# Adding partial products by accumulating transfers instead of on VectorE, in a kernel of attention beside a gated feed-forward network

## The chip, the core and the metric

The kernel runs on one core of one Trainium2 chip. The core has a matrix engine (TensorE, PE in the profile, with its weight loads as PEld), a vector engine (VectorE, DVE), an engine for functions of one input (ScalarE, ACT), a general engine (GpSimd, POOL) and an engine that issues transfers (SyncE, SP). Each engine takes its instructions in order. Transfers (DMAs) are issued by SP or by POOL here and run on 16 DMA engines that all queues share. The metric is the time of one execution on the device in microseconds; lower is better.

## The reference

The output is the sum of three things: the input `x`, an attention with a memory, and a gated feed-forward network, both on the layer-normalised input. There are 2048 tokens of width 448, 16 heads of width 28, four segments of 512 tokens, and 1792 hidden units.

```python
g = sigmoid(beta)
for s in range(4):                                   # segments of 512 tokens
    logits = qs @ ks.T * scale + mask
    a_dot = softmax(logits) @ vs
    a_mem = (phi(qs) @ M) / (phi(qs) @ z + 1e-6)      # phi(t) = t + 1 where t > 0, else exp(t)
    outs.append(g * a_mem + (1.0 - g) * a_dot)
    M = M + phi(ks).T @ vs
    z = z + phi(ks).sum(tokens)
attention = concat(outs) @ wo
gated = (sigmoid(xn @ w_gate) * (xn @ w_up)) @ w_down
return x + attention + gated                          # xn = layernorm(x)
```

The mask adds -1e9 where the key's place is before the query's.

## The kernel before

**Arithmetic.** All large products take operands that are split into a high and a low part, so one product of depth 448 is 11 matmuls (`TERMS`) and one of depth 128 is three. `acc[b]` holds, for block `b` of 512 tokens, first the input and then the running sum of the output: four tiles (`t`) of 128 tokens by 448.

**Phase 1, the front (L251 to L486).** It normalises, projects to queries, keys and values, writes them to DRAM (`qd`, `vd`), builds the memory `M`, and computes the memory's part of the attention in `recall` (L352): its result `tb` goes to `md[b]` in DRAM by a transfer that POOL issues (L358). The first steps of the feed-forward network are already mixed in here. In the front the order of PE, ACT and DVE is the program's own (`FRONT`, L51).

**Phase 2, the feed-forward network beside the attention.** From here on only PE's order is written by hand (`MANUAL`, L50). The order of ACT, DVE, POOL and SP is chosen by the framework's scheduler when the program is built, and each then runs in that fixed order. PE alternates steps of two generators: `gated` and `attention`.

- `gated` (L147) walks over the hidden units in pairs of 128-wide slices (`f0` = 0, 2, ..., 12, seven pairs), and for each pair over the four blocks `b`. For one pair and block it makes four *slots*: gate and up product of each slice (L224, 11 matmuls each). After a slice's two products ACT and DVE form the hidden values `hh` (L232 to L237).
- `down` (L149) multiplies the two slices' `hh` by their down weights: for each of the four token tiles six matmuls (L154) into one PSUM bank, three for the first slice and then three for the second. Then DVE adds the bank to `acc` (L157). The four `down` of one pair and block are put in the list `todo` (L244) and one is taken after each slot, two slots late. The banks alternate between `pd` and one of the two `gu`, so one kind comes back every second `down`.
- Weights come by SP: `load_up` (L162) into `raw` (one buffer, 512 KB), `load_down` (L166) into `rawd` (two buffers, 224 KB each). `ready_up` (L170) and `ready_down` (L174) split them: ACT copies the high part (L82), DVE subtracts to get the low part (L83). A buffer is free for the next load once DVE has read it. `wdn` has four buffers in the pool `late`, which exists only after the front. So the first two `ready_down` are held back in `begin` (L188) and issued at L491. The dictionary `ahead` (L201 to L215) says after which block and slot the later loads and splits are issued.
- `attention` (L618) works on pairs of heads (`Pair`): PE makes scores (L522), ACT copies them out (L525), POOL masks (L534), DVE takes maxima (L537) and subtracts (L573), ACT takes the exponential (L574). `Unit.finish` (L593) multiplies four heads' weights by the values (L599), turns the result (L606) and weighs it (L125) into `on`. For segments after the first, POOL adds the memory's part `tb` (L611), which SP has loaded from `md` (`load_memory`, L588 to L591). POOL then issues the transfer of `on` to `od` (L612).

**Phase 3, the output projection (`project`, L653).** `od` is loaded, turned and multiplied by `wo`; DVE adds to `acc` (L685), and the sum is stored.

Of the kernel before, what the change touches and what calls it, by code (L numbers as in the profile page):

```python
# [9 lines left out]
F32 = mybir.dt.float32  # L10
F32R = mybir.dt.float32r
AF = mybir.ActivationFunctionType
ALU = mybir.AluOpType
# [3 lines left out]
P = 128  # L17
D = 448
# [3 lines left out]
NB = 4  # L22
L = 512
NT = 4
# [9 lines left out]
FG = 2  # L34
# [22 lines left out]
def kernel(  # L57
# [69 lines left out]
    qd = [dram.tile([2 * D, 2, L], F32, name=f"qd{b}") for b in range(NB)]  # L127
    fd = [dram.tile([D, L], F32, name=f"fd{b}") for b in range(NB)]
    vd = [dram.tile([P, NT, H * 32], F32, name=f"vd{b}") for b in range(NB)]
    md = [dram.tile([P, NT, D], F32, name=f"md{b}") for b in range(NB)]  # L130
    od = [dram.tile([P, NT, D], F32, name=f"od{b}") for b in range(NB)]

    mid = ctx.enter_context(tc.tile_pool(name="mid", bufs=3, reuse_waits="tile"))
# [12 lines left out]

    def gated():  # L147

        def down(b, hs, wd, t, tag="pd"):  # L149
            tok = slice(t * P, (t + 1) * P)  # L150
            mms = [(h[:, a, tok], wd[f][:, w, :]) for f, h in hs for a, w in ((0, 0), (0, 1), (1, 0))]
            pd = bank("pd", tag)
            for n, (l, r) in enumerate(mms):
                T.matmul(pd[:, :D], l, r, start=n == 0, stop=n == len(mms) - 1)  # L154
                if n == 2:
                    yield
            V.tensor_add(acc[b][:, t, :], pd[:, :D], acc[b][:, t, :])  # L157
            yield

        raw_up, raw_down, wgu, wdn = {}, {}, {}, {}  # L160

        def load_up(f):  # L162
            raw_up[f] = mid.tile([P, 1024], F32, name="raw", bufs=1)
            nc.sync.dma_start(raw_up[f], w_ffn[f][:, :1024])

        def load_down(f):  # L166
            raw_down[f] = mid.tile([P, D], F32, name="rawd", bufs=2)
            nc.sync.dma_start(raw_down[f], w_ffn[f][:, 1024:])

        def ready_up(f):  # L170
            wgu[f] = eight_k(F32R, "wgu")
            split_weights(wgu[f], raw_up[f].rearrange("p (c n) -> p c n", c=4))

        def ready_down(f):  # L174
            wdn[f] = late[0].tile([P, 2, D], F32R, name="wdn", bufs=4)
            split(wdn[f][:, 0, :], wdn[f][:, 1, :], raw_down[f])

        raw_o = {}

        def load_out(h):  # L180
            raw_o[h] = mid.tile([P, 1024], F32, name="raw", bufs=1)[:, :2 * D]
            nc.sync.dma_start(raw_o[h], w_o[:, 2 * D * h:2 * D * (h + 1)])

        def ready_out(h):
            wo[h] = eight_k(F32R, "wo").rearrange("p c n -> p (c n)")
            split(wo[h][:, :2 * D], wo[h][:, 2 * D:4 * D], raw_o[h])

        begin.append(lambda: (ready_down(0), ready_down(1)))  # L188
        load_up(0)
        yield  # L190
        ready_up(0)
        load_up(1)
        load_down(0)
        load_down(1)
        yield


        todo = [None, None]
        for f0 in range(0, NF, FG):

            ahead = {}  # L201
            if f0 == 0:
                ahead[0, 0] = lambda: ready_up(1)
            if f0 + FG < NF:
                ahead[0, 2] = lambda: load_up(f0 + 2)
                ahead[1, 2] = lambda: (ready_up(f0 + 2), load_down(f0 + 2))
                ahead[1, 3] = lambda: load_up(f0 + 3)
                ahead[2, 1] = lambda: (ready_down(f0 + 2), load_down(f0 + 3))
                ahead[3, 2] = lambda: ready_up(f0 + 3)
                ahead[3, 3] = lambda: ready_down(f0 + 3)  # L210
            else:

                ahead[0, 2] = lambda: load_out(0)
                ahead[1, 2] = lambda: (ready_out(0), load_out(1))
                ahead[3, 2] = lambda: ready_out(1)  # L215
            for b in range(NB):
                hs = []
                for f in range(f0, f0 + FG):
                    pgu = []
                    for side in range(2):  # L220
                        slot = 2 * (f - f0) + side
                        dst = bank("pgu", ("gu", "p")[side])
                        for n, (a, w) in enumerate(TERMS):
                            T.matmul(dst, wgu[f][:, w, side * P:(side + 1) * P], xs[b][:, a, :],  # L224
                                     start=n == 0, stop=n == len(TERMS) - 1)
                            if n in (3, 7):
                                yield
                        pgu.append(dst)
                        if side == 1:

                            sg = two_k("sg")
                            A.activation(sg, pgu[0], AF.Tanh, scale=0.5)  # L232
                            V.scalar_tensor_tensor(sg, sg, 1.0, pgu[1], op0=ALU.add, op1=ALU.mult)  # L233
                            hh = four_k(F32R, "hh")
                            A.activation(hh[:, 0, :], sg, AF.Copy, scale=0.5)  # L235
                            V.scalar_tensor_tensor(hh[:, 1, :], sg, 0.5, hh[:, 0, :].bitcast(F32),  # L236
                                                   op0=ALU.mult, op1=ALU.subtract)  # L237
                            hs.append((f, hh))
                        yield
                        if todo and f0 + b > 0:  # L240
                            yield from todo.pop(0) or ()
                        if (b, slot) in ahead:
                            ahead[b, slot]()
                todo += [down(b, hs, wdn, t, ("pd", "gu")[t % 2]) for t in range(NT)]  # L244
        rest.extend(todo)


# [3 lines left out]
    with tc.tile_pool(name="front", bufs=2) as sb, tc.manual_schedule(engines=FRONT):  # L251
# [100 lines left out]
        def recall(b, i, phi):  # L352
            tb = sb.tile([P, NT * HG, DH], F32, name="tb", bufs=2)
            n2 = bank("n2", ("m", "pd")[i % 2] if b < NB - 1 else "m")
            for t in range(NT):
                T.matmul(n2[:, t * P:(t + 1) * P], phi[:, t * P:(t + 1) * P], mst[b % 2][i], start=True, stop=True)  # L356
            weigh(sb, tb, n2, gate[:, HG * i:HG * (i + 1)], MEM_EPS)
            nc.gpsimd.dma_start(md[b][:, :, GW * i:GW * (i + 1)], tb.rearrange("p (t j) d -> p t (j d)", t=NT))  # L358

        raw = [four_k(F32, "wv_raw") for _ in range(2)]  # L360
        raw = [raw[t // 2][:, t % 2, :D] for t in range(4)]
# [215 lines left out]
    class Unit:  # L577
# [7 lines left out]
            self.vv = sb.tile([P, NT, HG * 32], F32, name="vv")  # L585
            nc.sync.dma_start(self.vv, vd[self.s][:, :, self.i * P:(self.i + 1) * P])

        def load_memory(self):  # L588
            if self.s > 0:
                self.tb = sb.tile([P, NT, GW], F32, name="tb")  # L590
                nc.sync.dma_start(self.tb, md[self.s][:, :, GW * self.i:GW * (self.i + 1)])  # L591

        def finish(self):  # L593

            s, i = self.s, self.i
# [11 lines left out]
            on = sb.tile([P, NT * HG, DH], F32, name="on")  # L607
            weigh(sb, on, n1, gate_n[:, HG * i:HG * (i + 1)], 0.0)
            o3 = on.rearrange("p (t j) d -> p t (j d)", t=NT)
            if s > 0:  # L610
                G.tensor_add(o3, o3, self.tb)  # L611
            nc.gpsimd.dma_start(od[s][:, :, GW * i:GW * (i + 1)], o3)  # L612
            yield

    pairs = [Pair(n) for n in range(NB * H // 2)]
# [2 lines left out]
    def attention():  # L618
# [5 lines left out]
        for u in range(len(units) + 1):  # L624
            for n in range(2):
                run[n] = pairs[2 * u + n].scores() if u < len(units) else iter(())
            for k, which in enumerate(SLOT):
# [15 lines left out]
                if which == 2 and u > 0:  # L643
                    fin = units[u - 1].finish()
                    next(fin)
                    units[u - 1].load_memory()
                    if u < len(units):
                        units[u].load_values()
                if which == 3 and u > 0:
# [91 lines left out]
```

## Time and profile before

| what | value |
|---|---|
| time, median of 3 runs | 722.73 us (722.65 to 722.96) |
| time of the profiled execution | 723.55 us |
| its span, first to last instruction | 721.9 us |
| mean granted TensorE clock | 0.997 of full speed |
| DVE busy, of the span | 561.2 us (78%) |
| ACT busy | 337.7 us (47%) |
| POOL busy | 155.0 us (21%) |

The profile is of one execution that took 0.82 us longer than the median; 1.65 us of it lie outside the span. Its strip of 40 slices shows the span in equal parts of 18 us. A digit is the busy share in tenths, and a 9 means nine tenths or more:

```profile
DVE  6776776545888897888888898887898878889553
ACT  3635344233555555455555554544455553554220
POOL 4400020102213222222232422223132221231100
DMA  8533656677234213421234324242432234222242
```

The front ends near 170 us and phase 3 begins near 665 us. Between them DVE is busy for eight tenths or more of most slices, ACT for about five, POOL for two, and the DMA engines for three. A group's row gives line, engine, operation, tiles written and read, shape and count, then after the bar the busy time, the mean duration of one in ns, and the idle time of the engine just before them with what ended it.

### The profile page before, as it was taken

The numbers are of one execution on the slowest core, as the hardware profiler recorded it, in microseconds if no ns is written. First come the engines' busy times: TensorE is split into PE (matmuls) and PEld (weight loads), VectorE is DVE, ScalarE is ACT, GpSimd is POOL, SyncE is SP. The second block draws the span as 40 slices with busy tenths as digits, with TensorE's granted clock in tenths as the row PEclk, the third lists the DMA queues.
The fourth block names the chain that finished last, engine by engine and source line by source line (L and its number), as shares of the span: only waits on it lengthen the run. The fifth ranks groups of instructions, "written<-read, shape, count | busy, mean of one in ns | idle before, by whom it ended". The sixth has DMA issues, their size and how long they took to land.

```text
span 721.9 us, 10864 instructions
## 1 busy us (share of the span) xinstructions
PE 706.7 (98%) x3788; PEld 584.0 (81%) x3788; DVE 561.2 (78%) x1030; ACT 337.7 (47%) x552; POOL 155.0 (21%) x361
## 2 busy tenths in 40 slices
PE   7999999999999999999999999999899999999997
PEld 5788988887878787787877878778687777878797
DVE  6776776545888897888888898887898878889553
ACT  3635344233555555455555554544455553554220
POOL 4400020102213222222232422223132221231100
PEclk9999999999999999999999999999999999999999
DMA  8533656677234213421234324242432234222242
GB/s 295 234 147 146 218 192 228 216 259 205 65 77 118 85 52 96 121 77 54 64 109 120 91 57 119 81 116 65 83 93 78 70 78 115 64 74 85 97 147 90
DMA packets 52902, 86.24 MB, mean 119 GB/s; under 512 B 13936, under 2 KB 31024, under 8 KB 52336
## 3 DMA queue, kind: packets, MB, share of 16 engines
q1 hardware_dynamic: 50608, 79.13, 35.6%
q0 software_dynamic: 2240, 6.42, 2.7%
q8 instruction: 30, 0.49, 0.3%
q14 instruction: 24, 0.20, 0.1%
HBM read 53.81 MB, written 31.72 MB: 118 GB/s over the span
## 4 chain that ended last, share of the span: by engine, by line
PE 54%; DVE 23%; issue 10%; POOL 6%; ACT 3%; DMA 2%; SPq 1%; POOLq 0%; ACTq 0%; DVEq 0%
PE pgu L224 17%; PE pd L154 9%; PE pp L310 8%; DVE mx L537 5%; PE po L681 5%; PE pv L299 4%; DVE w L573 4%; DVE mb L565 3%; POOL w L534 3%; DVE acc L157 2%; PE st L522 2%; PE pa L599 2%; POOL on L611 2%; PE n L356 2%; PE pmm L338 1%
## 5 line engine op out<-in xcount | busy, mean ns | idle before, releaser
L224 PE MATMUL pgu<-xs,wgu 128*128 128x512 f32 x1232 | 322.5, 399 | 0.0
L224 PEld LDWEIGHTS pgu<-xs,wgu 128*128 128x128 f32 x1232 | 226.6, 189 | 45.1 <-issue 1.8
L154 PE MATMUL pd<-wdn,hh 128*128 128x448 f32 x672 | 164.7, 371 | 1.9 <-ACT wdn L82 1.0
L154 PEld LDWEIGHTS pd<-wdn,hh 128*128 128x128 f32 x672 | 122.5, 189 | 17.8 <-ACT wdn L82 1.4
L574 ACT ACTIVATE w<-w 128x1024 f32<-128x1024 f32 (+1 forms) x96 | 87.0, 915 | 89.2 <-DVE w L573 80.3
L534 POOL TENSOR_SCALAR_AFFINE_SELECT w<-w 128x256 f32<-128x256 f32 (+1 forms) x160 | 72.4, 456 | 235.6 <-ACT w L525 232.2
L537 DVE TRANSPOSE_TENSOR_REDUCE mx<-w 128x32 f32<-128x1024 f32 (+1 forms) x96 | 101.0, 1056 | 23.8 <-POOL w L534 23.7
L525 ACT ACTIVATE w<-st 128x512 f32<-128x512 f32 x160 | 93.2, 588 | 54.4 <-PE st L522 54.0
L573 DVE TENSOR_TENSOR w<-w,mb 128x1024 f32<-128x1024 f32 (+3 forms) x128 | 108.3, 869 | 0.4
L310 PE MATMUL pp<-xs,wqk 128*128 128x512 f32 x308 | 77.3, 399 | 0.0
L157 DVE TENSOR_TENSOR acc<-pd,acc 128x448 f32<-128x448 f32 x112 | 67.7, 606 | 4.0 <-PE pd L154 4.0
L522 PE MATMUL st<-qk 84*128 84x128 f32 (+3 forms) x256 | 64.5, 313 | 2.1 <-ACT w L525 2.1
L310 PEld LDWEIGHTS pp<-xs,wqk 128*128 128x128 f32 x308 | 56.7, 189 | 11.8
L235 ACT ACTIVATE hh<-sg 128x512 fp32r<-128x512 f32 x56 | 35.1, 627 | 52.8 <-DVE sg L233 45.9
L522 PEld LDWEIGHTS st<-qk 84*128 84x128 f32 x256 | 48.5, 189 | 11.9 <-ACT w L525 3.6
L565 DVE STREAM_TRANSPOSE mb<-top 128x1024 f32<-128x1024 f32 x32 | 39.8, 1243 | 15.2 <-POOL top L562 15.1
L232 ACT ACTIVATE sg<-pgu 128x512 f32<-128x512 f32 x56 | 33.1, 591 | 24.3 <-PE pgu L224 24.2
L316 DVE TENSOR_TENSOR qk<-pp,qk 128x512 fp32r<-128x512 f32 x28 | 19.4, 691 | 30.7 <-ACT e L315 23.6
L236 DVE SCALAR_TENSOR_TENSOR hh<-sg,hh 128x512 fp32r<-128x512 f32 x56 | 39.7, 709 | 4.2 <-ACT hh L235 3.9
L299 PE MATMUL pv<-wv,xs 128*128 128x448 f32 x176 | 39.0, 372 | 2.5 <-ACT xs L98 2.0
L311 ACT ACTIVATE qk<-pp 128x512 fp32r<-128x512 f32 x28 | 16.7, 597 | 50.8 <-PE pp L310 36.6
L233 DVE SCALAR_TENSOR_TENSOR sg<-sg,pgu 128x512 f32<-128x512 f32 x56 | 37.3, 667 | 4.0 <-PE pgu L224 3.9
(95 smaller groups left out, 650.0 us busy)
## 6 DMA issues: line engine op xcount, KB each, us to landing
qk<-qd SPq DMA_DIRECT2D x192, 112.0 KB
qd<-qk SPq DMA_DIRECT2D x28, 512.0 KB
raw<-in_w_ffn SPq DMA_DIRECT2D x14, 512.0 KB
vd<-vst SPq DMA_DIRECT2D x4, 1024.0 KB
vv<-vd SPq DMA_DIRECT2D x16, 256.0 KB
od<-on POOLq DMA_DIRECT2D x16, 224.0 KB, 3.7
ob<-od SPq DMA_DIRECT2D x4, 896.0 KB
out<-acc SPq DMA_DIRECT2D x16, 224.0 KB
```

The costliest lines, as they stand in the source:

```text
L154: T.matmul(pd[:, :D], l, r, start=n == 0, stop=n == len(mms) - 1)
L157: V.tensor_add(acc[b][:, t, :], pd[:, :D], acc[b][:, t, :])
L224: T.matmul(dst, wgu[f][:, w, side * P:(side + 1) * P], xs[b][:, a, :], start=n == 0, stop=n == len(TERMS) - 1)
L299: T.matmul(pv[:, :D], xs[b][:, a, t * P:(t + 1) * P], wv[:, w, :], start=n == 0, stop=n == len(TERMS) - 1)
L310: T.matmul(pp, wqk[c][:, w, :], xs[b][:, a, :], start=n == 0, stop=n == len(TERMS) - 1)
L522: T.matmul(st[:, at:at + L - kb * P], self.qk[:KS, 1, h, kb * P:(kb + 1) * P], self.qk[:KS, 0, h, kb * P:], start=True, stop=True)
L525: A.activation(w, st, AF.Copy)
L534: G.affine_select(d, d, pattern=pattern, base=0, channel_multiplier=-1, compare_op=ALU.is_ge, fill=MASK)
L537: V.tensor_reduce(mx[:, 16 * n0:16 * (n + 1)], self.w[:, n0 * L:(n + 1) * L].rearrange("p (b n) -> p b n", n=32), axis=mybir.AxisListType. ...
L565: V.transpose(mb.rearrange("p h (b n) -> p (h b) n", n=32), top.rearrange("p h b -> p (h b)").unsqueeze(2).to_broadcast([P, 32, 32]))
L573: V.tensor_sub(w[:, :, a:b], w[:, :, a:b], mb[:, :, q0:])
L574: A.activation(w, w, AF.Exp, scale=SCALE)
```

## The change

- `down` gets an argument `add`. For the middle five of the seven pairs (`0 < f0 < NF - FG`, that is `f0` = 2 to 10) it is POOL. Then ACT copies the bank to a new tile `part` in SBUF (two buffers), and POOL issues a transfer that adds `part` to `acc`. For the first and last pair DVE adds as before.
- `rawd` has one buffer instead of two. At the start of phase 2 only slice 0's down weights are made ready, and slice 1's load is issued then. They are made ready after block 1's slot 1.
- The memory's part is written to `od` itself instead of `md`. Attention's part is then added to it in DRAM by the transfer that stores it, for every segment but the first. The load of the memory's part and POOL's addition go away.

```diff
-    md = [dram.tile([P, NT, D], F32, name=f"md{b}") for b in range(NB)]
...
-        def down(b, hs, wd, t, tag="pd"):
+        def down(b, hs, wd, t, tag="pd", add=V):
...
-            V.tensor_add(acc[b][:, t, :], pd[:, :D], acc[b][:, t, :])
+            if add is V:
+                V.tensor_add(acc[b][:, t, :], pd[:, :D], acc[b][:, t, :])
+            else:
+                part = late[0].tile([P, D], F32, name="part", bufs=2)
+                A.activation(part, pd[:, :D], AF.Copy)
+                add.dma_start(acc[b][:, t, :], part, accum_op=ALU.add)
             yield
...
-            raw_down[f] = mid.tile([P, D], F32, name="rawd", bufs=2)
+            raw_down[f] = mid.tile([P, D], F32, name="rawd", bufs=1)
...
-        begin.append(lambda: (ready_down(0), ready_down(1)))
+        begin.append(lambda: (ready_down(0), load_down(1)))
...
         load_down(0)
-        load_down(1)
...
                 ahead[0, 0] = lambda: ready_up(1)
+                ahead[1, 1] = lambda: ready_down(1)
...
-                todo += [down(b, hs, wdn, t, ("pd", "gu")[t % 2]) for t in range(NT)]
+                add = G if 0 < f0 < NF - FG else V
+                todo += [down(b, hs, wdn, t, ("pd", "gu")[t % 2], add) for t in range(NT)]
...
-            nc.gpsimd.dma_start(md[b][:, :, GW * i:GW * (i + 1)], tb.rearrange("p (t j) d -> p t (j d)", t=NT))
+            nc.gpsimd.dma_start(od[b][:, :, GW * i:GW * (i + 1)], tb.rearrange("p (t j) d -> p t (j d)", t=NT))
...
-        def load_memory(self):
-            if self.s > 0:
-                self.tb = sb.tile([P, NT, GW], F32, name="tb")
-                nc.sync.dma_start(self.tb, md[self.s][:, :, GW * self.i:GW * (self.i + 1)])
...
-            if s > 0:
-                G.tensor_add(o3, o3, self.tb)
-            nc.gpsimd.dma_start(od[s][:, :, GW * i:GW * (i + 1)], o3)
+            nc.gpsimd.dma_start(od[s][:, :, GW * i:GW * (i + 1)], o3, accum_op=ALU.add if s > 0 else ALU.bypass)
...
-                    units[u - 1].load_memory()
```

## The prediction

> **What bounds the kernel now.** I read the page's busy times first, then the waits of PE, then the timeline around each wait. In every row a bracket is the engine's idle time before it and what ended it.
>
> ```profile
> span 721.9 us, 10864 instructions
> PE 706.7 (98%) x3788; PEld 584.0 (81%) x3788; DVE 561.2 (78%) x1030; ACT 337.7 (47%) x552; POOL 155.0 (21%) x361
> ```
>
> and the waits of PE between 160 and 690 us (total, times, longest):
>
> ```profile
> PE st L522 <- ACT w L525: 2.1, 3, 0.8
> PE n L606 <- ACT w L602: 2.1, 1, 2.1
> PE pd L154 <- ACT wdn L82: 1.0, 1, 1.0
> ...
> PE pd L154 <- DVE wdn L83: 0.2, 1, 0.2
> ```
>
> PE is busy for 98% of the span, and its waits are few; the row left out lies in the output projection. The change leaves PE's instructions and their order, written by hand, as they are. So time can go only where PE stands idle or runs slow, and come only from new standstills. DVE's 78% is no bound by itself. Here are the standstills of the middle, each beside the matmuls before it:
>
> ```profile
> 413.98 2.73 PE L224 MATMUL pgu<-xs,wgu 128*128 128x512 f32 x11
> ```
>
> ```profile
> 437.61 2.02 PE L224 MATMUL pgu<-xs,wgu 128*128 128x512 f32 x8
> 438.09 1.06 ACT L82 ACTIVATE wgu<-raw 128x1024 fp32r<-128x1024 f32 x1 [3.99 <-DMA raw<-in_w_ffn]
> 440.21 0.50 PE L522 MATMUL st<-qk 84*128 84x512 f32 x1 [0.57 <-ACT w L525]
> ...
> 514.48 1.89 PE L224 MATMUL pgu<-xs,wgu 128*128 128x512 f32 x7
> 516.84 1.06 ACT L82 ACTIVATE wgu<-raw 128x1024 fp32r<-128x1024 f32 x1 [1.80 <-DMA raw<-in_w_ffn]
> 518.43 0.66 PE L606 MATMUL n<-ident,w 128*128 128x128 f32 x4 [2.06 <-ACT w L602]
> ...
> 591.65 1.80 PE L224 MATMUL pgu<-xs,wgu 128*128 128x512 f32 x7
> 592.20 0.95 ACT L82 ACTIVATE wo<-raw 128x896 fp32r<-128x896 f32 x1 [2.29 <-DMA raw<-in_w_o]
> 594.21 0.50 PE L522 MATMUL st<-qk 84*128 84x512 f32 x1 [0.75 <-ACT w L525]
> ```
>
> The 11 matmuls in 2.73 us, the last of which lasts 0.40, stand 0.233 us apart. By that pitch PE was due at 439.47, 516.1 and 593.28, and so lost **0.74, 2.3 and 0.93 us**. The three have one cause: ACT stood at the split of a weight that had not landed, and PE's copies stood behind it. The third of the waits for L525 comes in the last pair, whose adds stay on DVE. I leave it.
>
> The middle one has a second price. The window rows give PE, PEld, DVE, ACT and POOL busy, then PEclk:
>
> ```profile
> 516.14:519.55 3.41, 1.35 (x9) 1.08 (x9) 1.52 (x4) 2.03 (x3) 0.18 (x1) 1.00 1.00 166
> 519.55:522.97 3.42, 3.42 (x10) 2.84 (x9) 2.50 (x5) 0.60 (x1) 0.92 (x5) 0.50 0.28 43
> 171.43:174.84 3.41, 2.25 (x9) 1.35 (x8) 2.33 (x7) 2.01 (x4) 0.71 (x1) 1.00 0.67 180
> 245.00:612.00 367.00, 363.62 (x1951) 294.12 (x1951) 313.74 (x528) 190.35 (x300) 96.57 (x241) 1.00 0.32 87
> ```
>
> After 3.41 us in which PE was busy for 1.35, it was granted half the clock for 3.42 us, half of which, **1.7 us**, is lost. After 2.25 of 3.41 it was not. So the middle holds 0.74 + 2.3 + 0.93 + 1.7 = **5.7 us** that the change could win.
>
> **The change part by part.**
>
> *DVE's adds.* Five pairs times four blocks times four tiles are 80 adds, 80 x 0.606 = 48 us off DVE; ACT gets 80 copies of the same shape out of PSUM, 80 x 0.542 = 43 us:
>
> ```profile
> L157 DVE TENSOR_TENSOR acc<-pd,acc 128x448 f32<-128x448 f32 x112 | 67.7, 606 | 4.0 <-PE pd L154 4.0
> L301 ACT ACTIVATE vst<-pv 128x448 f32<-128x448 f32 x16 | 8.7, 542 | 25.4 <-PE pv L299 25.4
> ```
>
> and a part of the chain of waits that ended in PE's 2.3 us:
>
> ```profile
> 505.39 0.53 DVE acc L157
> ...
> 509.98 0.54 DVE acc L157
> ...
> 511.71 5.10 DMA raw<-in_w_ffn
> ```
>
> These adds fall about into the stretch from 245 to 612 us. There DVE goes from 313.7 to 313.7 - 48 = 266 of 367 us (72%), ACT from 190.4 to 190.4 + 43 = 233 (64%). In that chain SP could reload the one `raw` only after DVE's L83, and two adds stood before that. They alone give 1.07 us back there, and less idling then probably keeps the clock: 1.07 + 1.7 = 2.8. The lower bound of the gain, with 0.5 each at the other two, is 3.8. The upper is all 5.7, because the whole DVE queue gets shorter. Against it, ACT carries 12 points more; I allow one new wait of the usual 0.9 us. I take **-4.8**.
>
> *POOL* issues 80 transfers more and loses 12 additions:
>
> ```profile
> L612 POOL DMA_DIRECT2D od<-on x16: 724/724/727, 222.1 to 675.6; - x16
> L611 POOL TENSOR_TENSOR on<-on,tb 128x448 f32<-128x448 f32 x12 | 16.2, 1346 | 42.0 <-DVE on L125 41.9
> POOL w L534 <- ACT w L525: 175.4, 79, 5.6
> DMA to landing us min/median/max: 2.5/3.7/5.6
> q0 software_dynamic: 2240, 6.42, 2.7%
> ```
>
> 80 x 0.724 = 58 us; 16.2 go. In the middle POOL reaches about 96.6 + 58 - 16 = 138 of 367 us. An adding transfer has no row. Its issue I bound by 0.7 and twice that, its landing by 2.5 and twice 3.7 = 7.4, and take 0.72 and 3.7, the same size plain. Each new issue waits for ACT's copy, and the mask L534 queues behind it. POOL stood 175 us there anyway, so this costs nothing unless POOL fills; DVE's maxima wait for the masks. Two `part` buffers turn over once per two `down`, 2 x 367/80 = 9.2 us, against POOL's mean wait 175.4/79 = 2.2, + 0.72 + 3.7 = 6.6 us: hidden. The next add to the same tile of `acc` comes 16 `down` later, 16 x 4.6 = 73 us, against a landing of at most 7.4: hidden. ACT's copy waits for the same six matmuls as the add did; behind it stand the score copies L525, whose banks PE needs next. Where the copy comes late, its own bank has the same 9.2 us. The 28 plain transfers of q0 took 2.7% of the span on 16 engines, 0.7 us each; 80 more add 56 us, 15 points on 0.32 (30 if adding reads and writes twice): hidden, as nothing waits for bandwidth but the weights.
>
> *Memory's part.* 12 SP loads at L591 go, and with them SP's waits there, nothing of it on PE's path: the late weight's issue waited for DVE (the chain above). The last store must land before the projection loads it, and does:
>
> ```profile
> 675.59 0.72 POOL L612 DMA_DIRECT2D od<-on  x1 [0.29 <-POOL on L611]
> 688.18 0.53 SPq L658 DMA_DIRECT2D ob<-od  x1
> ```
>
> 12.6 us of cover against at most 7.4. Zero.
>
> *The start of the down weights* is where the change costs:
>
> ```profile
> 172.84 0.62 DVE L125 TENSOR_TENSOR tb<-n,rc 128x448 f32<-128x448 f32 x1 [0.61 <-DMA md<-tb]
> 173.27 1.03 ACT L82 ACTIVATE wdn<-rawd 128x448 fp32r<-128x448 f32 x2
> 173.87 1.16 DVE L83 TENSOR_TENSOR wdn<-rawd,wdn 128x448 fp32r<-128x448 f32 x2 [0.40 <-ACT wdn L82]
> ...
> 174.55 1.28 PE L154 MATMUL pd<-wdn,hh 128*128 128x448 f32 x5 [0.19 <-DVE wdn L83]
> ...
> 175.66 0.40 PE L522 MATMUL st<-qk 84*128 84x384 f32 x2
> ```
>
> ```profile
> 434.51 3.50 DMA raw<-in_w_ffn
> ```
>
> PE already waits here for the first split (1.0 + 0.2 above). Now both slices' raw weights lie ready. After the change slice 1's load needs the one buffer, free when DVE's first L83 ends, at 174.5. That L83 can't move up by more than 0.4, since the front's order puts L125 before it, to 173.46. The load's landing has no row of its own: 2.5 us (the shortest of that size) to 3.5 (twice the size, at 434.51); I take 2.7, nearer its size, so 177.2. ACT's copy is half of 1.03 to 1.16, 0.57: 177.8. DVE's half, 0.62 with its start: 178.45. The first `down` needs the low part in its fifth matmul and has one more after it, 0.2 us each: it ends at 178.85 instead of 175.66, **+3.2 us** (2.6 to 4.0). `ahead` being later in the program doesn't help: the data are not there. Nothing covers this, because PE's next steps are fixed behind it. The later single loads, each 2.7 and a split of 1.2 us, have a pair's 73 us as cover: zero.
>
> In that hole PE runs four matmuls of 0.2 in about 5.5 us, emptier than the 1.35 in 3.41 that halved the clock: **+1.7**.
>
> The sum: 721.9 + 3.2 + 1.7 - 4.8 = 722.0 of span, or 723.65 with the 1.65 outside it, against 723.55 profiled. On the median: 722.73 + 0.1 = **722.8 us**.
>
> **The rivals.**
>
> *Faster: the hole at the start keeps the clock, and no new wait comes.* 722.73 + 3.2 - 5.7 = **720.2**. Against it stands the window at 516.14. The Trainium skill, page "TensorE: Matmul & The Clock Gate", section "Why this matters for your kernels", asks only that gaps stay under about 3 us; by that, a hole of 2.7 us would keep the clock, and the sum would be 721.1. The trace disagrees, with a gap of 2.06 us before the half clock.
>
> *Faster by more: the load comes earlier than I think* (another buffer order, ACT's split before the front's end), the start costs nothing: 722.73 - 4.8 = **717.9**. Against it: L125 ahead of L83.
>
> *Slower: `part` becomes the bound.* Where an adding transfer lands after more than 9.2 - 2.2 - 0.72 = 6.3 us, ACT's copy waits for its buffer with the score copies L525 behind it. At POOL's longest wait, 5.6, that is already so from 2.9 us. PE then loses about 0.9 as at 594. Five to ten such events: 722.8 + 4.5 to 9, **727 to 732**. For it: the longest waits exist. Against: most are near 2.2.
>
> *Slower: it doesn't do what it says.* The middle's waits stay, because `raw` itself lands late (3.50 and 5.10 us, by more DMA traffic later still) and ACT's own load replaces DVE's: 722.73 + 4.9 = **727.6**.
>
> **How the numbers follow.** Forecast 0.42 (own range 721.3 to 724.2); clock kept 0.20; load hidden 0.07; `part` 0.15; waits stay 0.16. About 0.2%, 1.45 us, is what a measurement of this kernel can tell from no change. Faster 0.20 + 0.07 = 0.27, same 0.42, slower 0.15 + 0.16 = 0.31. The range 719.5 to 728.5 leaves out the hidden load and the worse half of `part`, some 0.15.
>
> **What would show it.** Right: PE idle near 175 to 178 behind a late second `rawd`, PEclk 0.50 after it, L157 at 32, DVE near 72% between 245 and 612, ACT's waits for `raw` gone. Wrong: no hole near 175; PE waiting for L525 while ACT waits for `part`; issues or landings of the adding transfers far above 0.72 and 3.7 us.

## The result and the profile after

The changed kernel takes 741.99 us (median of 4 runs, 740.98 to 744.53) where the kernel before takes 722.69 us beside it. The ratio is 1.027 (95% interval 1.0245 to 1.0296). It is slower by 19 us, and outside the predicted range of 719.5 to 728.5 us. The profiled execution took 740.98 us; its span is 17.4 us longer than before.

From the page of the changed kernel, the busy times:

```profile
PE 710.7 (96%) x3788; PEld 586.1 (79%) x3788; DVE 515.2 (70%) x950; ACT 371.8 (50%) x632; POOL 212.9 (29%) x429
```

DVE has lost 46 us and ACT has won 34, as meant. POOL went from 155.0 to 212.9 us. PE still has its 3788 matmuls, but stands more. Its waits between 160 and 700 us:

```profile
PE st L528 <- DMA qk<-qd: 8.2, 1, 8.2
PE st L528 <- ACT w L531: 7.5, 7, 2.2
PE n L607 <- ACT w L603: 3.0, 2, 2.2
```

(Of the two shorter rows behind these, 0.7 and 0.3 us, the first lies in the output projection, as before. The lines have moved: scores L528, their copies L531, masks L540, maxima L543, `down` L153, its copy L160, its transfer L161, loads of down weights L172.) Before, the waits for ACT's score copies were 2.1 us in 3; now they are 7.5 in 7. And there is a wait of 8.2 us that was not there at all.

**The start.** The timeline of SP, ACT and PE in the changed kernel:

```profile
161.72 0.40 SPq L512 DMA_DIRECT2D qk<-qd  x1
174.82 0.35 SPq L172 DMA_DIRECT2D rawd<-in_w_ffn  x1
175.22 4.85 SPq L512 DMA_DIRECT2D qk<-qd  x11
...
177.43 0.58 ACT L82 ACTIVATE wdn<-rawd 128x448 fp32r<-128x448 f32 x1 [3.29 <-DMA rawd<-in_w_ffn]
...
181.14 0.76 PE L528 MATMUL st<-qk 84*128 84x512 f32 x1 [8.16 <-DMA qk<-qd]
```

its windows there (us, then PE, PEld, DVE, ACT and POOL busy, then PEclk):

```profile
178.20:181.70 3.50, 0.56 (x1) 0.50 (x2) 0.46 (x1) 0.00 (x0) 0.00 (x0) 0.50 0.92 217
181.70:184.60 2.90, 2.90 (x10) 2.63 (x9) 0.42 (x1) 0.60 (x1) 0.29 (x1) 0.50 1.02 235
184.60:187.50 2.90, 2.90 (x8) 2.28 (x8) 1.45 (x2) 0.60 (x1) 0.41 (x1) 0.53 0.10 36
```

and SP in the kernel before:

```profile
161.42 7.32 SPq L506 DMA_DIRECT2D qk<-qd  x12
```

Before, SP issued the 12 loads of the first scores' operands one behind the other from 161.42. Now the scheduler has put slice 1's load behind the first of them. That load must wait until DVE has read slice 0's raw weights, at 174.8, and the other 11 wait in the queue behind it. Slice 1's split comes at 177.43, almost when the prediction had it (177.2 landed). But by then PE waits for something else, until 181.14. It then has half the clock for some 6 us, most of it in the last two rows. That is 8.16 us, less the 1.2 us that PE waited here before, and 2.9 x 0.5 + 2.9 x 0.47 = 2.8 us by the clock: 9.8 us, by this working.

**The middle.** The window of 245 to 612 us, whose counterpart the prediction shows (the changed kernel is some 10 us behind in it), and the longest wait of the middle, followed back through the timelines of POOL, DVE, ACT and PE:

```profile
245.00:612.00 367.00, 358.02 (x1924) 287.43 (x1923) 267.50 (x441) 221.25 (x375) 149.26 (x296) 1.00 0.60 125
```

```profile
527.47 0.87 POOL L161 DMA_DIRECT2D acc<-part  x1 [2.63 <-ACT w L531]
528.05 1.07 POOL L540 TENSOR_SCALAR_AFFINE_SELECT w<-w 128x256 f32<-128x256 f32 x2
528.80 1.25 DVE L543 TRANSPOSE_TENSOR_REDUCE mx<-w 128x32 f32<-128x1024 f32 x1 [1.96 <-POOL w L540]
529.97 0.65 DVE L237 SCALAR_TENSOR_TENSOR sg<-sg,pgu 128x512 f32<-128x512 f32 x1
530.66 0.63 ACT L239 ACTIVATE hh<-sg 128x512 fp32r<-128x512 f32 x1 [2.47 <-DVE sg L237]
...
532.56 0.59 ACT L603 ACTIVATE w<-pa 128x512 f32<-128x512 f32 x1
533.20 0.66 PE L607 MATMUL n<-ident,w 128*128 128x128 f32 x4 [2.21 <-ACT w L603]
```

DVE's 267.5 and ACT's 221.25 us are about as predicted (266 and 233). PE's busy time fell from 363.62 to 358.02, though nobody is full. The chain says how: a transfer stands first in POOL's queue, two masks come behind it (rows on POOL are rough and overlap here), DVE's maxima wait for the masks, the next step of the hidden values waits in DVE's queue behind the maxima, ACT waits for that, and behind it in ACT's queue, after a copy to `part` and a weight's split, stands the copy that PE needs. No step is long; each engine takes its instructions in order, so one delay goes through four queues.

The matmul at the end of this chain waited before, too: it is the one at 518.43, which waited 2.06 us for a weight's split. The wait is about as long as it was, with another cause: in e4_copy below, which has the copies but no transfers, it is gone. Eight other waits of the middle, 6.5 us together, stand at matmuls that did not wait before.

### The profile page after: what moved, and what is told of

The parts are those of the page before. It is cut to its first block, busy times and chain, and to the rows that moved or that the text cites. A ratio compares the mean times of both kernels' runs of the same rounds, so it can differ in the third digit from the quotient of the medians.

```text
span 739.3 us, 11058 instructions
## 1 busy us (share of the span) xinstructions
PE 710.7 (96%) x3788; PEld 586.1 (79%) x3788; DVE 515.2 (70%) x950; ACT 371.8 (50%) x632; POOL 212.9 (29%) x429
## 3 DMA queue, kind: packets, MB, share of 16 engines
q0 software_dynamic: 19136, 24.78, 20.4%
## 4 chain that ended last, share of the span: by engine, by line
PE 56%; issue 16%; DVE 12%; POOL 9%; ACT 4%; DMA 2%; SPq 1%; POOLq 0%; ACTq 0%; DVEq 0%
PE pgu L228 19%; PE pd L153 9%; PE pp L316 8%; PE po L679 5%; PE pv L305 5%; POOL w L540 4%; DVE mx L543 3%; PE st L528 3%; POOL acc L161 2%; DVE w L579 2%; PE pa L600 2%; PE n L362 1%; DVE mb L571 1%; PE pmm L344 1%; ACT w L580 1%
## 5 line engine op out<-in xcount | busy, mean ns | idle before, releaser
L153 PE MATMUL pd<-wdn,hh 128*128 128x448 f32 x672 | 165.6, 373 | 0.7 <-DVE acc L683 0.7
L543 DVE TRANSPOSE_TENSOR_REDUCE mx<-w 128x32 f32<-128x1024 f32 (+1 forms) x96 | 101.6, 1061 | 59.5 <-POOL w L540 59.5
L153 PEld LDWEIGHTS pd<-wdn,hh 128*128 128x128 f32 x672 | 123.6, 190 | 16.2 <-issue 1.2
L540 POOL TENSOR_SCALAR_AFFINE_SELECT w<-w 128x256 f32<-128x256 f32 (+1 forms) x160 | 79.3, 506 | 130.4 <-ACT w L531 127.9
L531 ACT ACTIVATE w<-st 128x512 f32<-128x512 f32 x160 | 94.8, 594 | 40.8 <-PE st L528 40.4
L579 DVE TENSOR_TENSOR w<-w,mb 128x1024 f32<-128x1024 f32 (+3 forms) x128 | 101.6, 818 | 0.6
L161 POOL DMA_DIRECT2D acc<-part x80 | 70.6, 883 | 96.2 <-ACT part L160 88.9
L528 PE MATMUL st<-qk 84*128 84x128 f32 (+3 forms) x256 | 65.6, 317 | 15.7 <-DMA qk<-qd 8.2
L528 PEld LDWEIGHTS st<-qk 84*128 84x128 f32 x256 | 48.9, 191 | 28.5 <-ACT w L531 11.7
L571 DVE STREAM_TRANSPOSE mb<-top 128x1024 f32<-128x1024 f32 x32 | 39.9, 1246 | 19.3 <-POOL top L568 19.2
L160 ACT ACTIVATE part<-pd 128x448 f32<-128x448 f32 x80 | 43.1, 539 | 6.2 <-PE pd L153 3.2
```

The costliest lines, as they stand in the source:

```text
L161: add.dma_start(acc[b][:, t, :], part, accum_op=ALU.add)
L528: T.matmul(st[:, at:at + L - kb * P], self.qk[:KS, 1, h, kb * P:(kb + 1) * P], self.qk[:KS, 0, h, kb * P:], start=True, stop=True)
L531: A.activation(w, st, AF.Copy)
L540: G.affine_select(d, d, pattern=pattern, base=0, channel_multiplier=-1, compare_op=ALU.is_ge, fill=MASK)
L543: V.tensor_reduce(mx[:, 16 * n0:16 * (n + 1)], self.w[:, n0 * L:(n + 1) * L].rearrange("p (b n) -> p b n", n=32), axis=mybir.AxisListType. ...
L571: V.transpose(mb.rearrange("p h (b n) -> p (h b) n", n=32), top.rearrange("p h b -> p (h b)").unsqueeze(2).to_broadcast([P, 32, 32]))
```

## The experiments

All kernels have PE's 3788 matmuls in the same order. So beside the times I give PE's *lag*: the start of a certain matmul less its start in the kernel before, each in its profiled execution. What a stretch costs is the lag at its end less the lag at its beginning. "Start" is from the 878th matmul (170 us in the kernel before) to the 917th (180 us), "middle" from there to the 3578th (680 us).

| kernel | median us | start | middle |
|---|---|---|---|
| changed kernel | 741.99 | +9.6 | +7.8 |
| e1_start | 729.18 | +9.2 | -3.6 |
| e2_mid_store | 733.27 | 0.0 | +10.0 |
| e3_store | 719.06 | 0.0 | -4.8 |
| e6_behind | 738.62 | +5.8 | +8.5 |
| e4_copy | 722.93 | 0.0 | -1.9 |
| e5_plain | 726.38 | 0.0 | +1.3 |
| e7_const | 777.34 | 0.0 | +53.4 |
| e8_later | 733.04 | 0.0 | +12.0 |
| e10_pool_only | 733.26 | 0.0 | +10.2 |
| e11_pool_order | 734.25 | 0.0 | +9.9 |
| e12_pool_order_later | 745.50 | 0.0 | +19.3 |
| e13_half_rows | 732.92 | 0.0 | +9.2 |
| e14_pool_order_step | 730.17 | 0.0 | +5.3 |
| e15_masks | 732.67 | 0.0 | +11.1 |
| e16_store_masks | 719.41 | 0.0 | -4.4 |

The kernel before took 722.0 to 722.6 us beside them.

### The start, and the parts one by one

**e1_start** is the kernel before with only the lines of the down weights' start changed:

```diff
-            raw_down[f] = mid.tile([P, D], F32, name="rawd", bufs=2)
+            raw_down[f] = mid.tile([P, D], F32, name="rawd", bufs=1)
...
-        begin.append(lambda: (ready_down(0), ready_down(1)))
+        begin.append(lambda: (ready_down(0), load_down(1)))
...
-        load_down(1)
...
+                ahead[1, 1] = lambda: ready_down(1)
```

> The kernel before with only the start of the down weights changed (one rawd buffer, slice 1's load behind slice 0's split, its split one block later). Theory Queue (SP's queue stands behind the waiting load with 11 of the 12 first qk loads behind it): PE idle about 8.2 us at its first score matmul near 181 and about 2.9 us lost to the half clock, less the 1.6 us that stood there before, so 722.7 + 9.7 = about 732. Rival Landing (only the late landing of slice 1 itself costs, as the prediction had it): 722.7 + 4.9 = 727.6 at most. Rival Middle (the start costs nothing, all 19 us come later): 722.7.

729.18 us, ratio 1.0089 (1.0074 to 1.0104). The start costs 9.2 us, as Queue said: PE's wait for the operands is 7.9 us. The total is lower than expected, since the middle gave 3.6 us back, although of it only `rawd`'s second buffer was taken away. The orders of ACT, DVE and POOL are chosen anew at each build (here ACT's and DVE's differ from the kernel before's at places all along the middle), and PE's 2.1 us wait at 518 us fell to 0.7.

**e2_mid_store** is the changed kernel with slice 1's load put where it waits for nobody:

```diff
         def load_down(f):
-            raw_down[f] = mid.tile([P, D], F32, name="rawd", bufs=1)
+            raw_down[f] = (late[0].tile([P, D], F32, name="part", bufs=2) if f == 1 else
+                           mid.tile([P, D], F32, name="rawd", bufs=1))
...
-        begin.append(lambda: (ready_down(0), load_down(1)))
+        begin.append(lambda: (load_down(1), ready_down(0), ready_down(1)))
...
-                ahead[1, 1] = lambda: ready_down(1)
```

> The changed kernel, but slice 1's raw down weight is loaded into a buffer of part, so that its load waits for no split and both splits come first as before. The order of POOL is that of the changed kernel, those of DVE and ACT differ from it only at the start. Theory Queue: the 8 us hole near 181 goes, the middle keeps its new waits: 742.0 - 9.7 = about 732. Rival Landing: 742.0 - 4.9 = about 737. Rival Middle: 742.

733.27 us, ratio 1.0147 (1.0132 to 1.0162). The start is free, and 8.7 us of the 19 are gone. SP in this kernel:

```profile
161.06 0.38 SPq L173 DMA_DIRECT2D part<-in_w_ffn  x1
161.55 6.61 SPq L512 DMA_DIRECT2D qk<-qd  x12
```

**e6_behind** keeps the waiting load, but behind the 12 loads:

```diff
-        begin.append(lambda: (ready_down(0), load_down(1)))
+        begin.append(lambda: ready_down(0))
+        begin.append(lambda: load_down(1))
...
         next(steps)
+        begin[1]()
```

> The changed kernel, but slice 1's load stands behind all 12 first qk loads in SP's queue; it still waits for slice 0's split, with one rawd buffer. Theory Queue: the hole at the first score matmul near 181 goes; what stays at the start is the late landing of slice 1, priced by the prediction at 3.2 + 1.7 us: 742.0 - 9.7 + 4.9 = about 737, at best 732 if the split one block later hides it. Rival Landing (the hole is the load itself, wherever it stands in the queue): 742.

738.62 us, ratio 1.0228 (1.0211 to 1.0245). The hole at the first scores is gone, and what is left at the start is what the prediction had priced: ACT gets slice 1 at 177.66, `down`'s fourth matmul waits, and a window of half clock follows (PE's timeline, then the window):

```profile
178.29 1.77 PE L153 MATMUL pd<-wdn,hh 128*128 128x448 f32 x3 [2.52 <-ACT wdn L82]
...
179.50:182.90 3.40, 3.40 (x10) 2.83 (x9) 1.89 (x3) 1.17 (x2) 0.41 (x1) 0.50 0.26 67
```

It costs 5.8 us of lag, against 3.2 + 1.7 predicted. So the load's own lateness is 5.8 of the 9.6 us, and the queue behind it the other 3.8.

**e3_store** leaves the start and the adds as before and has only the adding store of `od` (the lines of `md`, `load_memory` and POOL's addition go as in the change):

```diff
-            nc.gpsimd.dma_start(od[s][:, :, GW * i:GW * (i + 1)], o3)
+            nc.gpsimd.dma_start(od[s][:, :, GW * i:GW * (i + 1)], o3, accum_op=ALU.add if s > 0 else ALU.bypass)
```

> The kernel before with only the adding store of attention's part into the memory's in DRAM; the middle pairs' adds stay on DVE, the start as before. Theory (the prediction's term zero, the load of the memory's part and POOL's addition were beside PE's path): 722.7, within 0.3%. Rival (the issue of an adding store, 1.2 us on POOL where the plain one took 0.72, delays the masks, or the changed order of the queues moves the weights' loads): 724 to 727.

719.06 us, ratio 0.9952 (0.9935 to 0.9968): faster than both kernels. Neither expectation foresaw it. PE's waits in this kernel, between 160 and 690 us, have lost the one for ACT's L602 (2.1 us before; now L603), and with it the half clock. The longest that is left in the middle is 0.5 us, for a score copy.

The weights for which ACT had stood there now come 2.5 us earlier (SP and ACT; in the kernel before 511.71 and 516.84):

```profile
509.98 0.36 SPq L168 DMA_DIRECT2D raw<-in_w_ffn  x1
...
514.29 1.06 ACT L82 ACTIVATE wgu<-raw 128x1024 fp32r<-128x1024 f32 x1 [0.99 <-DMA raw<-in_w_ffn]
```

DVE reached the split before it (L83), which frees `raw`, at 508.70 in place of 510.44. A new order is not the reason: ACT's and DVE's instructions stand in the order of the kernel before up to 524 us, past the wait. What went is POOL's addition. DVE and POOL in the kernel before, and then in e3_store:

```profile
462.65 1.98 DVE L573 TENSOR_TENSOR w<-w,mb 128x256 f32<-128x256 f32 x2
462.81 1.26 POOL L611 TENSOR_TENSOR on<-on,tb 128x448 f32<-128x448 f32 x1 [0.47 <-DVE on L125]
...
465.04 0.49 POOL L534 TENSOR_SCALAR_AFFINE_SELECT w<-w 128x256 f32<-128x256 f32 x1
...
465.56 1.25 DVE L537 TRANSPOSE_TENSOR_REDUCE mx<-w 128x32 f32<-128x1024 f32 x1 [0.39 <-POOL w L534]
```

```profile
462.17 1.02 DVE L579 TENSOR_TENSOR w<-w,mb 128x256 f32<-128x256 f32 x2
462.55 1.20 POOL L611 DMA_DIRECT2D od<-on  x1 [0.68 <-DVE on L125]
463.23 0.95 POOL L540 TENSOR_SCALAR_AFFINE_SELECT w<-w 128x256 f32<-128x256 f32 x1
...
464.22 1.25 DVE L543 TRANSPOSE_TENSOR_REDUCE mx<-w 128x32 f32<-128x1024 f32 x1 [0.49 <-POOL w L540]
```

Without the addition the mask starts 1.8 us earlier, and DVE's two subtractions, which ran beside it, take 1.02 us in place of 1.98. DVE's maxima start 1.3 us earlier, and the lead lasts to the split. The additions were not taken out by themselves; e1_start lost most of the same wait in another way.

### The middle

From here on the start is as in e2_mid_store or as before, and the adding store is in. e4 (with one `part` buffer) and e5 change the lines behind the copy:

```diff
                 A.activation(part, pd[:, :D], AF.Copy)
-                add.dma_start(acc[b][:, t, :], part, accum_op=ALU.add)
```

```diff
-                add.dma_start(acc[b][:, t, :], part, accum_op=ALU.add)
+                add.dma_start(acc[b][:, t, :], part)
```

> The start as before, the adding store, and in the middle pairs ScalarE's copy without the transfer behind it (leaves out those pairs' adds to the sums). e2_mid_store took 733.3, e3_store 719.1, so the middle's transfers and copies cost 14.2. Theory Pool (the transfers' issues stand on POOL's queue, wait there for ACT's copy, and the masks behind them come late): 719 to 722. Rival Act (the 80 copies, 43 us more on ScalarE, stand ahead of the score copies and exponentials): 730 to 733. Rival Traffic (the adding transfers' reads and writes hold up the weights' and the scores' loads): 719 to 722 too; the next kernel tells it from Pool.

> As e2_mid_store, order of all queues the same, but the middle's transfers write over the sums instead of adding to them (leaves out those adds). Theory Pool: the wait for ACT's copy and the place on POOL stay, only the issue falls from 0.88 to about 0.72 us: 731 to 733. Rival Traffic (adding reads the destination too, twice the bytes): 726 or less.

722.93 and 726.38 us. That makes a ladder: 719.1 with the store alone, 722.9 with the copies on ACT in place of DVE's adds, 726.4 with plain transfers behind them, 733.3 with adding ones, 742.0 with the start. Act as the main cause falls: the copies cost 3.9 us, new orders included. Most of this stands in one place, where ACT's queue has a score copy behind two exponentials that wait for DVE (ACT and PE of e4_copy):

```profile
612.29 1.06 ACT L579 ACTIVATE w<-w 128x1024 f32<-128x1024 f32 x1 [5.18 <-DVE w L578]
...
615.12 1.06 ACT L579 ACTIVATE w<-w 128x1024 f32<-128x1024 f32 x1 [0.81 <-DVE w L578]
616.08 0.58 ACT L530 ACTIVATE w<-st 128x512 f32<-128x512 f32 x1
...
616.71 0.50 PE L527 MATMUL st<-qk 84*128 84x512 f32 x1 [2.58 <-ACT w L530]
```

The same matmul waits in the changed kernel, for 1.95 us.

The last step of 6.9 us was a miss for Pool: e5_plain and e2_mid_store have every queue in the same order, and only overwriting stands against adding. Some 3 us of the step stand at the wait followed back above: it is 0.43 us in e5_plain, and 2.20 us in e2_mid_store with a window of half clock behind it. From the page of the two, e5_plain first, the queue of POOL's transfers and POOL's row for the middle's issues (busy us, mean ns):

```profile
q0 software_dynamic: 12736, 24.78, 13.0%
...
L161 POOL DMA_DIRECT2D acc<-part x80 | 46.1, 577 | 96.9 <-ACT part L160 92.6
```

```profile
q0 software_dynamic: 19136, 24.78, 20.6%
...
L161 POOL DMA_DIRECT2D acc<-part x80 | 70.6, 883 | 97.5 <-ACT part L160 90.2
```

An issue takes 0.58 us plain and 0.88 adding, but the transfers differ too (13.0% and 20.6% of the engines' time). Two runs tell these apart:

```diff
-                add.dma_start(acc[b][:, t, :], part, accum_op=ALU.add)
+                add.tensor_add(part[:, :336], part[:, :336], part[:, :336])
```

```diff
-                add.dma_start(acc[b][:, t, :], part, accum_op=ALU.add)
+                add.dma_start(acc[b][:64, t, :], part[:64], accum_op=ALU.add)
```

> As e2_mid_store, but in place of each middle transfer GpSimd does an addition of 336 columns of part to itself, about 0.85 us, behind the same wait for ScalarE's copy: POOL's wait and time without any transfer (leaves out the middle's adds). Theory Pool (POOL's time and waits cost the 14 us): 730 to 735, near e2_mid_store's 733.3. Rival Traffic (the adding transfers' packets hold up other loads): 722 to 725, near e4_copy's 722.9.

> As e2_mid_store, order of the queues the same, but each middle transfer adds only 64 of the 128 rows (leaves out the other half of these adds). Where the issue's time on POOL goes with the rows (0.88 to about 0.5 us): near e5_plain's 726.4, since that run had the same order and 0.58 us. Where the issue's time stays near 0.88 and the transfers' bytes don't matter: 733.

733.26 and 732.92 us. The same rows of e10_pool_only's page, and then of e13_half_rows':

```profile
q0 software_dynamic: 7616, 6.42, 5.7%
...
L161 POOL TENSOR_TENSOR part<-part 128x336 f32<-128x336 f32 x80 | 66.9, 837 | 81.7 <-ACT part L160 80.2
```

```profile
q0 software_dynamic: 14016, 15.60, 15.9%
...
L161 POOL DMA_DIRECT2D acc<-part x80 | 66.9, 836 | 94.7 <-ACT part L160 89.4
```

With no transfer at all, but 0.84 us on POOL in the same place, the time is that of e2_mid_store. With half the bytes but 0.84 us of issue, too. So the transfers' traffic costs nothing that can be seen here, and what this step costs is POOL's longer time for each of them. e13_half_rows says it more strongly, with every queue in e2_mid_store's order; e10_pool_only has other orders on DVE and ACT, and DVE is busy for 523.6 us there against 515.2. The Trainium skill, page "Perfetto Trace Analysis", section "DMA Instruction — SWDGE (GPSIMD)", says that such a row shows GpSimd's processors writing descriptors, and ends before the data have moved. The runs agree as far as the row's length hardly changes with the bytes (0.88 and 0.84 us).

Is it the wait, or the time? The next runs went at this, and not all of them reached it.

**e7_const** took the transfer from a constant tile (`zero[0]` in place of `part`), to be rid of the wait.

> As e2_mid_store, but the middle's 80 adding transfers take a constant tile of zeros and so wait for no copy of ScalarE; the copies stay (leaves out the middle's adds). POOL's order shifts with it. Theory Pool by the wait: POOL's wait at the issue (88.9 us in the changed kernel) goes, the masks come on time, the 80 x 0.88 us of issuing stay: 722 to 726. Rival Pool by the issue's time alone: 731 to 733. Rival Traffic: 731 to 733.

777.34 us. With nothing to wait for, the scheduler moved the transfers forward, and all 80 are issued between 177 and 312 us. 52 of the 54 us are lost up to the matmul that starts at 260 us in the kernel before, while POOL stood at issues for the landing of earlier ones (idle 44.3 us before them). From the matmul at 300 us there, its lag goes as e4_copy's does (-3.3 and -2.8 us to the end of the middle). It says nothing of the wait.

**e8_later** and **e12_pool_order_later** issue each transfer one `down` later, e12 with POOL in the program's order; **e11_pool_order** is e12's reference, **e14_pool_order_step** defers by one step of PE's order only. (In e8 and e12 one that is left over is issued before DVE's next add.)

```diff
-MANUAL = {mybir.EngineType.PE}
+MANUAL = {mybir.EngineType.PE, mybir.EngineType.Pool}
...
-                add.dma_start(acc[b][:, t, :], part, accum_op=ALU.add)
+                held.append((acc[b][:, t, :], part))
+                if len(held) > 1:
+                    add.dma_start(*held.pop(0), accum_op=ALU.add)
```

(in e14 the second part, behind the `yield` in the loop over `TERMS`)

```diff
                             if n in (3, 7):
                                 yield
+                                while held:
+                                    G.dma_start(*held.pop(0), accum_op=ALU.add)
```

> As e2_mid_store and whole, but each middle transfer is written one down product later in the program, behind the next copy, so that its copy is done when POOL comes to it. Theory Pool by the wait: 722 to 727 where POOL's order follows; POOL's wait for the copy falls to under a third of 88.9 us. Rival Pool by the issue's time, Act or Traffic: 731 to 733. A new wait of ACT's copy for a part buffer could take it back; then ACT's waits show it.

> As e2_mid_store and whole, but POOL keeps the order of the program, as PE does, where the planner ordered it before: the reference for the next one. The order changes little (146 lines of difference). 731 to 736 by every theory.

> As e11_pool_order, but each transfer one down product later in the program, which here fixes its place on POOL (in e8_later the planner had moved it back, so that run told nothing of the wait). Theory Pool by the wait: POOL's wait for ACT's copy falls to under a third and the time by 6 to 10 us against e11. Rival Pool by the issue's time (80 x 0.88 us on POOL and the slower masks beside them) or Traffic: within 3 us of e11.

> As e11_pool_order (734.3), whole, but each middle transfer is written one step of PE's order later (one to two us, where e12_pool_order_later took a whole down product). Theory Pool by the wait: POOL's wait for ACT's copy falls to under half of 65.9 us, ACT's wait for a part buffer stays under 10 us, and the time falls to 726 to 730. Rival Pool by the issue's time: the wait falls and the time stays within 2 us of 734.

e8_later: 733.04 us. The scheduler moved the transfers back to nearly the same places, so nothing changed. e11: 734.25 us. e12: 745.50 us, ratio 1.0316 (1.0294 to 1.0338) against e11's 1.0154 (1.0127 to 1.0182). Waits of POOL and of ACT in e12, 245 to 625 us:

```profile
POOL acc L165 <- ACT part L162: 4.9, 2, 2.5
...
ACT part L162 <- DMA acc<-part: 49.4, 23, 5.2
```

POOL's wait is gone, but with two `part` buffers ACT's copies now wait for the transfers, with the score copies behind them. That is the rival of the prediction in which `part` becomes the bound, brought about by this edit. It costs 11 us, where the time was to fall by 6 to 10; in the changed kernel itself this wait is 0.6 us, once. e14 lies between (730.17 us, ratio 1.0111, 1.0094 to 1.0128):

```profile
POOL acc L233 <- ACT part L160: 15.1, 13, 4.1
...
ACT part L160 <- DMA acc<-part: 12.4, 8, 3.8
```

POOL's wait fell from e11's 65.9 us to 15.1, and the time by 4.1, to just above the 726 to 730 expected; ACT's wait for `part` is 12.4 us, above the 10 expected. So a part of the cost may be the wait. It is not shown: the two intervals just touch, and e14 has other orders on DVE and ACT than e11.

**e15_masks** moves the 64 masks of one diagonal block each from POOL to DVE, and **e16_store_masks** does so without the transfers.

```diff
-                G.affine_select(d, d, pattern=pattern, base=0, channel_multiplier=-1, compare_op=ALU.is_ge, fill=MASK)
+                if pattern == [[1, P]]:
+                    V.tensor_add(d, d, low[0])
+                else:
+                    G.affine_select(d, d, pattern=pattern, base=0, channel_multiplier=-1, compare_op=ALU.is_ge, fill=MASK)
```

> As e2_mid_store (733.3) and whole, but the 64 masks of one diagonal block each (31 us of POOL) become additions of a constant on DVE, which has room in the middle (267 of 370 us). The transfers and their waits stay. Theory Pool (whichever part): POOL has 31 us less, and these masks no longer stand behind an issue: 722 to 728. Rival Act (the copies ahead of the score copies): 731 to 733.

> Control for e15_masks: e3_store (719.1; the adding store alone) with the same 64 masks on DVE. By Pool, POOL wasn't full there, and DVE, at 315 of 370 us, gets some 15 us more: 719 to 721. If it is faster than 719.1, the masks were late on POOL even without the transfers.

732.67 and 719.41 us. e15 is a miss: POOL has 26 us less to do and the time stays. POOL's wait for the copy, 87.0 us in e2_mid_store in the same window, has grown by 24 us:

```profile
POOL acc L162 <- ACT part L161: 111.1, 54, 6.0
```

POOL was not full, so room on it was worth nothing here; it only stands longer at the next issue, and the masks that are left still stand behind the issues. e16_store_masks came as expected, within 0.4 us of e3_store: without the middle's transfers, moving these masks off POOL gained nothing.

What stays open: how much of the 14.2 us between e3_store and e2_mid_store is the wait, how much the 0.88 us behind it, and how much the new orders. Of the middle's kernels only e5_plain and e13_half_rows have all queues in the order of e2_mid_store; the others have other orders on ACT, DVE or POOL too (e8_later at a few places only), and in e1_start new orders, with one `rawd` buffer less, moved the middle by 3.6 us.

## Why the prediction was wrong

**The start: the step that failed is "+3.2 (2.6 to 4.0)".** It took the late load's own way (landing 177.2, ACT 177.8) as what ends last. That way was right to half a microsecond: ACT's split began at 177.43 in the changed kernel. But the load was put on SP, where it waits 13 us for a buffer, and the step did not ask what stands behind it there: 11 loads for the first scores. e6_behind has the step as the prediction meant it, at 5.8 us with the clock (predicted 4.9); the queue adds 3.8.

**The clock, +1.7:** right in kind, and 2.8 us in size, since the hole was longer. In e6_behind a gap of 2.52 us was followed by 3.4 us at 0.50. The Trainium skill, page "TensorE: Matmul & The Clock Gate", section "Why this matters for your kernels", would have let that gap pass (under about 3 us); this run, like the kernel before, speaks against it. But a gap's length does not decide by itself. In the changed kernel one of 2.21 us, before 533.20, kept the clock, and in e13_half_rows even one of 3.29 us did, from 597.28 to 600.57:

```profile
595.52:598.93 3.41, 1.77 (x9) 1.10 (x7) 0.00 (x0) 0.36 (x1) 0.00 (x0) 1.00 0.25 48
598.93:602.34 3.41, 1.77 (x8) 1.62 (x9) 2.49 (x3) 3.41 (x7) 1.75 (x3) 1.00 0.18 37
602.34:605.76 3.42, 3.42 (x17) 2.86 (x16) 1.96 (x8) 1.19 (x3) 1.48 (x6) 1.00 0.96 256
```

The windows are counted in steps of 3.41 us back from 626.24, where this run's clock was halved. The gap fell across two of them, and PE was busy for 1.77 us in each; with 1.35 us in the kernel before, and 1.15 us in e6_behind's window that ends where its clock falls (177.57), the next was at half. So the prediction read the clock by the right thing, PE's busy time in a window. Where a hole falls among the windows is luck, and it did not count that.

**The middle's waits, -4.8: failed.** DVE's queue got 46 us lighter as worked out, and the step took the upper bound of the gain, 5.7, less the 0.9 it allowed. But of the three waits only the one at 440 us is gone in the changed kernel. The one at 518 us is as long as before, without the half clock; the one at 594 us grew from 0.75 to 2.18 us, as ACT waits there 4.4 us for a raw weight (2.3 before), and now has the half clock behind it. The wait at 518 us and its half clock, 4 of the 5.7 us to be won, go away wholly in e3_store and for the larger part in e1_start, which leave the adds alone; so a lighter DVE was not needed for it. And in the changed kernel seven waits for the score copies and two for L603 stand in the place of three and one.

**POOL, "this costs nothing unless POOL fills": failed, and it is the larger mistake.** POOL did not fill (149 of 367 us; 138 predicted), and it cost PE's path all the same: 6.9 us for issues of 0.88 in place of 0.58 us with every queue in the same order, and 3.5 us for the plain issues, new orders included. The prediction even named the queue, with the mask behind the issue and DVE's maxima behind the mask, and then priced it by POOL's share. The issue of 0.724 us was 0.883, inside its bounds, and the landing (3.6 against 3.7) and `part`'s turn-over were as predicted.

**ACT's copies**, allowed 0.9 us within the -4.8, took 3.9 in the ladder, new orders included.

**Memory's part, "Zero":** -3.6 us in the ladder. This failed for the same reason as POOL's term. The additions, 1.35 us each, stood on POOL ahead of masks, and so delayed DVE's split and the reload of `raw`, for which ACT and then PE waited at 518 us. The prediction had this late weight wait for DVE, and did not ask what DVE had waited for.

The ladder, whose steps add up by construction, is -3.6 (store) + 3.9 (copies) + 3.5 (plain issues) + 6.9 (adding) + 8.7 (start) = 19.4, against 19.3 measured. The rivals named two of these mechanisms, `part` and new waits on ACT, at the wrong place or size, and none of them a queue behind a waiting transfer.

## What to carry to other kernels

A transfer that must wait, for a buffer or for another engine's copy, holds up what is queued behind it on its issuing engine, and so does the time of its issue. So list that queue and follow it to the engine that sets the end, and don't price it by the issuing engine's busy share. An instruction that looks off the path, like POOL's additions here, may stand ahead of one that is on it. Where a scheduler orders the queues, an edit can also reorder them far from its own place, as in e1_start. So the parts of a change are worth timing one by one, as here the store alone was faster than the whole change and than the kernel before.

## What the runs showed of the hardware

- The issue of a transfer on GpSimd for one tile of 128 x 448 took 0.577 us plain and 0.883 us adding, and 0.836 us adding with half the rows. So it hardly goes with the bytes. An adding transfer is 144 packets, or 80 with half the rows, and a plain one 64: q0 has 19136, 12736 and 7616 packets with adding, plain and no transfers, 80 of them (14016 with half the rows).
- GpSimd's masks beside adding issues were slower: 503 ns on average in e2_mid_store, 443 in e5_plain with the same orders. Other kernels tell it less clearly: 456 in the kernel before and 464 in e3_store, without such issues in the middle, and 471 in e7_const with 80 of them.
- An adding store to DRAM (`od`) took 1.13 us to issue on average in the changed kernel, 12 of 16 adding; the plain ones 0.724.
